# A gated mix taken in one piece, longer transfer times for a list scheduler, one weight ring for two stages, and constants set up earlier

## The chip, the cores and the metric

The kernel runs on one core of one Trainium2 chip. A core has five engines with instruction queues of their own: TensorE (PE, matmuls), VectorE (DVE), ScalarE (ACT), GpSimd (POOL) and SyncE (SP, here used only to issue transfers), and 16 DMA engines that all transfers share. The metric is the device time of one execution in microseconds (us), lower is better.

## The reference

Two branches over the same 2048 tokens of 640 values are mixed by a gate per token. Branch A is attention with a sliding window of 256 and 32 heads of 20. Branch B is a recurrence: 64 segments of 32 tokens, each with 8 memory tokens in front, 32 heads of 192, and the memory rows of one segment's output are the memory of the next.

```python
g = _sigmoid((x * gate_w).sum(-1, keepdims=True))
a = _A_ref(x, A_wqkv, A_wo)          # sliding window attention
b = _B_ref(x, B_mem0, B_Wq, B_Wk, B_Wv, B_Wo, B_seg_len)
return g * a + (1 - g) * b

# in _B_ref
for s in range(n_seg):               # 64 segments, one after the other
    h = jnp.concatenate([mem, xs], axis=1)            # 8 + 32 rows
    q = jnp.einsum('btd,dhe->bhte', h, Wq)            # k and v alike
    ...                                               # masked softmax of 40 x 40 per head
    o = jnp.einsum('bhte,hed->btd', o, Wo)
    mem = o[:, :M, :].copy()
    outs.append(o[:, M:, :])
```

## The kernel before

The program has three stages. Branch A comes first and writes its gated result `ga` to DRAM (`ga_dram`), and 1 - g (`omg`) too. The tail (`tail_projections`) then projects the last 8 tokens of all segments at once with the weights of branch B, and stores them in `xin` in DRAM. Then come 64 steps (`branch_B`), one for each segment, each of which needs the memory rows of the step before.

The four weight matrices of branch B are cut into 80 pieces of 128 x 1536 (384 KB). 58 of them stay in SBUF for good ("resident"), and 22 are read again in every step ("streamed"). `EARLY` = 33 of the resident pieces are loaded during branch A, the next 19 during the tail, and `LAST` = 6 after the tail, by ACT's queue. The streamed pieces go through a ring of `RING` = 5 buffers: SP issues a load as soon as PE has finished with the piece that held the buffer. The tail has a ring of its own (`t_ring`, 4 buffers), the steps another (`b_w`, tiles `t_w`).

The order of the steps' instructions is set by `Sched`: PE's order is written out in `STEP`, and all other operations are put in the order in which a list scheduler with durations and latencies (`LAT`, in ns) would start them. Each engine then runs its instructions in that order, and waits on semaphores for what is not ready. Transfers of the steps, except those of weights, are all issued by POOL (`hT` is a segment's input, `xqk` and `xv` are the tail's projections for it, `ga` is branch A's result).

`store(s)` is the place where the step's result is mixed. PE transposes the output of segment s (`ox`), in the middle of step s + 1; DVE mixes it with `ga` in two halves of 320 columns, and there is one buffer for `ga`:

```python
for h in range(2):
    ga, c = sc.buf("ga"), h * D // 2
    sc.op("DMA", ... dma_start(tile_of(ga)[:], ga_dram[rows, cols]), writes=[ga])   # L949
    def f_r(): nc.vector.scalar_tensor_tensor(out=ga["tile"][:], in0=ox..., in1=ga["tile"][:], ...)  # L952
    sc.op("DVE", dve(320), f_r, reads=[ox], writes=[ga])
    sc.op("DMA", ... dma_start(outf[rows, cols], ga["tile"][:]), reads=[ga])        # L955
```

So the load of one half writes the buffer that the store of the half before still reads. Other lines that the prediction speaks of: L728 projections, L873 spread of the probabilities (`PTm`, which PE's `ps_pv` at L889 needs), L917 output projection (`ps_o`), L927 the memory rows copied into the next step's input (`t_hT`, the end of one step and the start of the next), L548 and L571 matmuls of the tail, L320 and L1044 the store and the load of `omg`.

Of the kernel before, what the change touches and what calls it, by code (L numbers as in the profile page):

```python
# [8 lines left out]
FP32 = mybir.dt.float32  # L9
# [5 lines left out]
SEG = 32  # L15
# [355 lines left out]
class Sched:  # L371
# [6 lines left out]
    LAT = {"PE": 190, "DVE": 125, "ACT": 140, "POOL": 150, "DMA": 2000, "SP": 2000}  # L378
# [140 lines left out]
def tail_projections(tc, weights, xTb, xin, late):  # L519
# [6 lines left out]
    with ExitStack() as ctx:  # L526
        ring = ctx.enter_context(tc.tile_pool(name="t_ring", bufs=4))
# [5 lines left out]
        def pieces(kind, g):  # L533
            return {m: weights.get(ring, (kind, g, m)) for m in weights.order(kind, g)}
# [64 lines left out]
def branch_B(ctx, tc, xin, mem0, weights, omg_sb, ga_dram, b_dram, outf):  # L599
    nc = tc.nc  # L600
    nseg = xin.shape[0]
    scale = float(192) ** -0.5

    const = ctx.enter_context(tc.tile_pool(name="b_const", bufs=1))
    sb = {
        "w": (RING, [P, PIECE]), "tok": (3, [P, 384]), "vtok": (2, [P, 384]), "K02": (2, [P, 4, 2, L]),
        "PTm": (2, [P, 2, 4, L]), "OT": (2, [P, 3, 4, L]), "Pm": (2, [P, 4, SEG]),
        "xqk": (1, [P, 4, 2, 12, MEM]), "xv": (1, [P, 384]), "ga": (1, [SEG, D // 2]), "hT": (2, [P, KT, SEG]),
    }
    kept = {"QT": (2, [P, 12 * L + 64 - L]), "Kz": (2, [P, 4, 2, L]), "Px": (4, [P, 64]), "PTx": (4, [P, 2, 4, 2, MEM]),  # L610
            "oT": (1, [P, KT * SEG + P - SEG])}
    ps = {"mm": 3, "tr": 2, "s": 2, "o": 1}
    pools = {t: ctx.enter_context(tc.tile_pool(name=f"b_{t}", bufs=n)) for t, (n, _) in sb.items()}
    pools |= {t: ctx.enter_context(tc.tile_pool(name=f"b_ps_{t}", bufs=n, space=bass.MemoryType.PSUM)) for t, n in ps.items()}
    stats = ctx.enter_context(tc.tile_pool(name="b_stats", bufs=3))
    still = {}
    for t, (n, shape) in kept.items():
# [7 lines left out]
    mask = const.tile([P, 4, L], BF, name="bmask")  # L625
    nc.gpsimd.memset(mask[:], 0.0)
    for a in range(2):
        mk = mask[64 * a:64 * a + 64]
        nc.gpsimd.affine_select(out=mk, in_=mk, compare_op=ALU.is_ge, fill=NEG, base=0,
                                pattern=[[0, 4], [-1, L]], channel_multiplier=1)  # L630
        nc.gpsimd.memset(mask[64 * a:64 * a + MEM], 0.0)
# [7 lines left out]
    mk_h = const.tile([P, 4, 4], FP32, name="mk_h")  # L639
# [10 lines left out]
    for a in range(2):  # L650
        nc.gpsimd.memset(mk_z[64 * a:64 * a + 64, a:a + 1], 1.0)

    sc = Sched({t: n for t, (n, _) in sb.items()} | {t: n for t, (n, _) in kept.items()} | ps)

    def tile_of(b, shape=None, dtype=BF, name=None):
        t = b["tag"]
        if b["tile"] is None:
            if t in kept:
                b["tile"] = still[t][b["n"] % kept[t][0]]
            elif t in sb:  # L660
                b["tile"] = pools[t].tile(sb[t][1], BF, name=f"t_{t}", tag=t)
# [129 lines left out]
    def scores(s, g):  # L791
# [21 lines left out]
        def f1():  # L813
            x["mx"] = stats.tile([P, 4], FP32, name="sm_mx")
# [121 lines left out]
    def store(s):  # L936
# [9 lines left out]
        for h in range(2):  # L946
            ga, c = sc.buf("ga"), h * D // 2
            rows, cols = slice(s * SEG, (s + 1) * SEG), slice(c, c + D // 2)
            sc.op("DMA", 500, lambda ga=ga, rows=rows, cols=cols: nc.gpsimd.dma_start(tile_of(ga)[:], ga_dram[rows, cols]), writes=[ga])  # L949

            def f_r(ga=ga, cols=cols):
                nc.vector.scalar_tensor_tensor(out=ga["tile"][:], in0=ox["tile"][0:SEG].rearrange("p k c -> p (k c)")[:, cols],  # L952
                                               scalar=omg_sb[:, s:s + 1], in1=ga["tile"][:], op0=ALU.mult, op1=ALU.add)
            sc.op("DVE", dve(320), f_r, reads=[ox], writes=[ga])
            sc.op("DMA", 500, lambda ga=ga, rows=rows, cols=cols: nc.gpsimd.dma_start(outf[rows, cols], ga["tile"][:]), reads=[ga])  # L955
# [20 lines left out]
EARLY = 33  # L976
LAST = 6
# [4 lines left out]
def kernel(  # L982
# [40 lines left out]
    units = [lambda u=u: weights.load_resident(pre, u, nc.sync) for u in early]  # L1023
    omg_sb = fin.tile([SEG, nseg], FP32, name="omg_sb")
    with tc.tile_pool(name="b_xtail", bufs=1) as xtail:
# [17 lines left out]
        with nc.allow_non_contiguous_dma(reason="tiny omg vector"):  # L1043
            nc.sync.dma_start(omg_sb[:], omg_dram[:].rearrange("(s t) -> t s", t=SEG))  # L1044
        post = wctx.enter_context(tc.tile_pool(name="b_post", bufs=1, side="right"))
        with tc.tile_pool(name="chk", bufs=1) as chk, tc.tile_pool(name="chk_ps", bufs=1, space=bass.MemoryType.PSUM) as chk_ps:
# [51 lines left out]
```

## Time and profile before

| | us |
|---|---|
| median of 3 runs (lowest, highest) | 2730.45 (2722.23, 2738.58) |
| the profiled execution | 2727.65 |
| its span, first to last instruction | 2725.9 |
| PE busy, share of the span | 2090.3 (77%) |
| DVE busy | 1051.0 (39%) |
| ACT busy | 923.3 (34%) |
| POOL busy | 579.8 (21%) |
| DMA, mean over the span | 238 GB/s, 649.37 MB |
| chain that ended last | DMA 47%, PE 27% |

An engine's busy time is an average over three stages with different limits, so it says little about what sets the end. The chain that ended last is followed back from the last instruction, at each step to what released it; transfers make up almost half of it, those of weights and, 10% each, the load and the store of the mix. The rows below take this apart by stage.

### The profile page before, as it was taken

What the parts mean: (1) busy time and instruction counts of PE and PEld (TensorE: products, weight loads), DVE (VectorE), ACT (ScalarE), POOL (GpSimd) and SP (SyncE); (2) the same over time, 40 slices, a digit from 0 to 9 for tenths busy, and PEclk for the clock granted to TensorE, in tenths of its full rate; (3) what the DMA queues carried; (4) which work ended last, traced back from release to release, by engine and by line L of the source; (5) the groups of instructions that cost most, each with busy time, mean ns of one, the idle gap of its engine ahead of it and who ended that gap; (6) DMA issues with size and microseconds to landing.
All of it is one profiled execution on the core that took longest, in us unless ns stands there. A gap on an engine that the chain in (4) does not pass through costs nothing.

```text
span 2725.9 us, 109560 instructions
## 1 busy us (share of the span) xinstructions
PE 2090.3 (77%) x48566; PEld 1569.8 (58%) x48566; DVE 1051.0 (39%) x3330; ACT 923.3 (34%) x1957; POOL 579.8 (21%) x1752
## 2 busy tenths in 40 slices
PE   7888879977777777777777777777777777777776
PEld 6777758555555555555555555555555555555554
DVE  5666633233333333333333333333333333333333
ACT  3555522233333333333333333333333333333332
POOL 3111101231222222222222222222222222222221
PEclk8777779998898899898888888898888888888888
DMA  3211165688788777788888788888777878888876
GB/s 122 64 60 59 54 179 147 176 304 269 270 270 269 271 271 270 270 275 270 273 282 276 266 272 275 268 284 279 268 271 267 269 271 267 283 271 268 274 266 207
DMA packets 256693, 649.37 MB, mean 238 GB/s; under 512 B 38730, under 2 KB 56274, under 8 KB 256210
## 3 DMA queue, kind: packets, MB, share of 16 engines
q1 hardware_dynamic: 224754, 589.03, 63.7%
q0 software_dynamic: 25216, 47.75, 6.0%
q8 instruction: 382, 6.26, 0.9%
q10 hardware_dynamic: 6240, 5.51, 0.7%
q14 instruction: 101, 0.83, 0.1%
HBM read 612.78 MB, written 29.37 MB: 236 GB/s over the span
## 4 chain that ended last, share of the span: by engine, by line
DMA 47%; PE 27%; issue 7%; POOL 3%; DVE 2%; SPq 0%; POOLq 0%; DVEq 0%; ACT 0%; ACTq 0%
DMA t_w<-in_B_Wq_dram 13%; DMA t_ga<-ga_dram 10%; DMA out_dram<-t_ga 10%; PE ps_o L917 9%; DMA t_w<-in_B_Wv_dram 8%; DMA t_w<-in_B_Wk_dram 5%; PE ps_q L728 5%; PE t_psum L548 4%; PE ps_v L728 3%; PE ps_pv L889 2%; PE ps_k L728 1%; DVE t_PTm L873 1%; POOL b_Kz L785 1%; PE S_ps L805 1%; POOL b_QT L764 1%
## 5 line engine op out<-in xcount | busy, mean ns | idle before, releaser
L728 PEld LDWEIGHTS <-t_hT 128*32 128x32 bf16 x15360 | 384.0, 97 | 390.5 <-issue 182.9
L889 PE MATMUL ps_pv<-t_PTm,t_vtok 128*64 128x160 bf16 x1536 | 117.5, 261 | 382.9 <-DVE t_PTm L873 382.9
L917 PE MATMUL ps_o<-t_OT,w_o 128*128 128x40 bf16 x10752 | 355.0, 190 | 6.1 <-issue 5.9
L900 ACT CAST t_OT<-ps_pv 128x480 bf16<-128x480 f32 x256 | 143.8, 562 | 624.2 <-PE ps_pv L896 623.9
L917 PEld LDWEIGHTS <-w_o 128*128 128x128 bf16 x10752 | 327.3, 103 | 30.7 <-issue 23.9
L889 PEld LDWEIGHTS <-t_vtok 128*64 128x64 bf16 x1536 | 73.7, 120 | 395.8 <-issue 393.4
L952 DVE SCALAR_TENSOR_TENSOR t_ga<-ox_ps,omg_sb,t_ga 32x320 bf16<-32x320 bf16 x128 | 68.4, 534 | 517.0 <-DMA t_ga<-ga_dram 511.3
L220 ACT ACTIVATE pt<-s_ps 128x1024 bf16<-128x1024 f32 x180 | 180.7, 1023 | 126.4 <-PE s_ps L217 126.3
L764 POOL COPY b_QT<-t_xqk 128x96 bf16<-128x96 bf16 x256 | 66.8, 261 | 736.8 <-PE S_ps L805 423.4
L728 PE MATMUL ps_q<-w_q,t_hT 128*32 128x384 bf16 x3584 | 199.5, 338 | 18.8 <-DVE t_hT L927 18.4
L728 PE MATMUL ps_k<-w_k,t_hT 128*32 128x384 bf16 x4096 | 212.9, 328 | 0.0
L774 DVE COPY t_K<-tr_k 128x256 bf16<-128x256 bf16 x256 | 74.6, 292 | 335.4 <-PE tr_k L751 329.1
L728 PE MATMUL ps_v<-w_v,t_hT 128*32 128x384 bf16 x3584 | 195.5, 332 | 0.1
L738 ACT CAST t_tok<-ps_q 128x384 bf16<-128x384 f32 x256 | 122.5, 479 | 201.0 <-PE ps_q L728 195.1
L917 PE MATMUL ps_o<-t_OT,t_w 128*128 128x40 bf16 x4608 | 175.1, 189 | 9.4 <-issue 8.5
L738 ACT CAST t_vtok<-ps_v 128x384 bf16<-128x384 f32 x256 | 122.5, 478 | 172.8 <-PE ps_v L728 172.6
L738 ACT CAST t_tok<-ps_k 128x384 bf16<-128x384 f32 x256 | 122.4, 478 | 158.4 <-PE ps_k L728 156.8
L751 PEld LDWEIGHTS <-t_tok 128*64 128x64 bf16 x3072 | 103.7, 110 | 104.1 <-issue 38.9
L917 PEld LDWEIGHTS <-t_w 128*128 128x128 bf16 x4608 | 151.7, 103 | 10.8 <-issue 9.4
L873 DVE TENSOR_TENSOR t_PTm<-PT_ps,mk_m 128x320 bf16<-128x320 f32 x256 | 122.9, 480 | 80.9 <-PE PT_ps L860 77.1
L728 PE MATMUL ps_q<-t_w,t_hT 128*32 128x384 bf16 x1536 | 119.6, 330 | 43.8 <-DMA t_w<-in_B_Wq_dram 42.8
L222 DVE TENSOR_TENSOR pt<-pt,pat 128x1024 bf16<-128x1024 bf16 x180 | 124.4, 691 | 74.5 <-ACT pt L220 71.8
(133 smaller groups left out, 3697.3 us busy)
## 6 DMA issues: line engine op xcount, KB each, us to landing
t_w<-in_B_Wq_dram SPq DMA_DIRECT2D x384, 384.0 KB, 5.0
t_w<-in_B_Wv_dram SPq DMA_DIRECT2D x384, 384.0 KB, 5.2
t_w<-in_B_Wo_dram SPq DMA_DIRECT2D x384, 384.0 KB, 5.2
t_w<-in_B_Wk_dram SPq DMA_DIRECT2D x256, 384.0 KB, 4.8
xin<-t_qk POOLq DMA_DIRECT2D x8, 1536.0 KB, 9.0
t_xqk<-xin POOLq DMA_DIRECT2D x64, 192.0 KB, 5.3
w_k<-in_B_Wk_dram SPq DMA_DIRECT2D x16, 384.0 KB, 4.0
t_xv<-xin POOLq DMA_DIRECT2D x64, 96.0 KB, 2.3
```

The lines of the kernel that those rows point to most:

```text
L220: nc.scalar.activation(out=pt, in_=sp[:], func=ACT.Exp, scale=scale)
L222: nc.vector.tensor_tensor(out=pt, in0=pt, in1=pat.unsqueeze(1).to_broadcast([P, 2, 512]), op=ALU.min)
L548: nc.tensor.matmul(pt[:, bb, :], lhsT=w[kt][:, c:c + P], rhs=xTb[:, kt, t0:t0 + HS * MEM], start=(x == 0), stop=(x == KT - 1))
L728: nc.tensor.matmul(t[32 * j:32 * j + 32, 0:384], lhsT=tile_of(hT)[:, kt, :], rhs=w[:, j * 384:(j + 1) * 384], start=(x == 0), stop=(x == K ...
L738: nc.scalar.copy(dst, src)
L751: nc.tensor.transpose(t[64 * a:64 * a + 64, k, :], tok["tile"][:, c:c + 64], ident[:], tile_position=(0, 64 * a))
L764: nc.gpsimd.tensor_copy(dst, tile_of(xqk)[:, g, 0, :, :])
L774: nc.vector.tensor_copy(tile_of(K02)[:, :, :, 0:SEG], src)
L873: nc.vector.tensor_tensor(out=tile_of(PTm)[:], in0=src.to_broadcast([P, 2, 4, L]), in1=mk_m[:].unsqueeze(1).unsqueeze(3).to_broadcast([P, ...
L889: nc.tensor.matmul(t[64 * a:64 * a + 64, 160 * b:160 * b + 160], lhsT=V["tile"][:, c:c + 64], rhs=PTm["tile"][:, a, :, :].rearrange("p j l ...
L900: sc.op("ACT", act(480), lambda: nc.scalar.copy(tile_of(OT)[:].rearrange("p b j l -> p (b j l)"), o["tile"][:, 0:480]), reads=[o], writes= ...
L917: nc.tensor.matmul(t[:, dt * L:(dt + 1) * L], lhsT=w_of("o", g, m, wb)[:, c:c + P], rhs=OT["tile"][:, b, i, :], start=(g == 0 and n == 0), ...
```

## The change

In a step, the mix is one operation over 640 columns in one buffer of that width, with one load and one store. `LAT` gives a transfer 5000 instead of 2000, and SP's weight loads 2500 instead of 2000. The tail and the steps share one ring of five buffers, created before branch A, and the streamed pieces of the first head group are loaded into it at the end of branch A (`first`). To make room, `EARLY` goes from 33 to 28 and `LAST` from 6 to 8, so that 22 resident pieces are loaded in the tail. The constants of the steps (zeroed buffers, identity, masks) are set up before the tail, not after it. The load of `omg` and the store of the range flag go from SP's queue to POOL's. The score mask is kept once and broadcast to the four heads, and three small softmax tiles become one with two buffers instead of three.

```diff
-    LAT = {"PE": 190, "DVE": 125, "ACT": 140, "POOL": 150, "DMA": 2000, "SP": 2000}
+    LAT = {"PE": 190, "DVE": 125, "ACT": 140, "POOL": 150, "DMA": 5000, "SP": 2500}
...
-def tail_projections(tc, weights, xTb, xin, late):
+def tail_projections(tc, weights, ring, first, xTb, xin, late):
...
-        ring = ctx.enter_context(tc.tile_pool(name="t_ring", bufs=4))
...
-            return {m: weights.get(ring, (kind, g, m)) for m in weights.order(kind, g)}
+            return {m: first.pop((kind, g, m), None) or weights.get(ring, (kind, g, m)) for m in weights.order(kind, g)}
...
+def step_constants(tc, const, tmp):
...
-    mask = const.tile([P, 4, L], BF, name="bmask")
+    mask = const.tile([P, 1, L], BF, name="bmask")
...
-        "xqk": (1, [P, 4, 2, 12, MEM]), "xv": (1, [P, 384]), "ga": (1, [SEG, D // 2]), "hT": (2, [P, KT, SEG]),
+        "xqk": (1, [P, 4, 2, 12, MEM]), "xv": (1, [P, 384]), "ga": (1, [SEG, D]), "hT": (2, [P, KT, SEG]),
...
+    pools["w"] = ring
...
-                nc.tensor.matmul(t[64 * a:64 * a + 64, 0:4 * L], lhsT=ident[:, 64 * a:64 * a + 64],
-                                 rhs=mask[:].rearrange("p j l -> p (j l)"), start=True, stop=False,
+                nc.tensor.matmul(t[64 * a:64 * a + 64, 0:4 * L].rearrange("p (j l) -> p j l", j=4), lhsT=ident[:, 64 * a:64 * a + 64],
+                                 rhs=mask[:].to_broadcast([P, 4, L]), start=True, stop=False,
...
-        for h in range(2):
-            ga, c = sc.buf("ga"), h * D // 2
-            rows, cols = slice(s * SEG, (s + 1) * SEG), slice(c, c + D // 2)
-            sc.op("DMA", 500, lambda ga=ga, rows=rows, cols=cols: nc.gpsimd.dma_start(tile_of(ga)[:], ga_dram[rows, cols]), writes=[ga])
...
-            sc.op("DVE", dve(320), f_r, reads=[ox], writes=[ga])
-            sc.op("DMA", 500, lambda ga=ga, rows=rows, cols=cols: nc.gpsimd.dma_start(outf[rows, cols], ga["tile"][:]), reads=[ga])
+        ga, rows = sc.buf("ga"), slice(s * SEG, (s + 1) * SEG)
+        sc.op("DMA", 500, lambda: nc.gpsimd.dma_start(tile_of(ga)[:], ga_dram[rows, :]), writes=[ga])
...
+        sc.op("DVE", dve(640), f_r, reads=[ox], writes=[ga])
+        sc.op("DMA", 500, lambda: nc.gpsimd.dma_start(outf[rows, :], ga["tile"][:]), reads=[ga])
...
-EARLY = 33
-LAST = 6
+EARLY = 28
+LAST = 8
...
+    ring = wctx.enter_context(tc.tile_pool(name="b_w", bufs=RING))
+    first = {}
+    ahead = [("q", 0, m) for m in range(5)] + [("k", 0, m) for m in range(5)]
+    ahead = [u for u in ahead if u in weights.streamed]
+
+    def load_first(u):
+        first[u] = weights.get(ring, u)
+    units += [lambda u=u: load_first(u) for u in ahead]
...
-            nc.sync.dma_start(omg_sb[:], omg_dram[:].rearrange("(s t) -> t s", t=SEG))
+            nc.gpsimd.dma_start(omg_sb[:], omg_dram[:].rearrange("(s t) -> t s", t=SEG))
...
+            step_c = step_constants(tc, bconst, chk)
...
-            nc.sync.dma_start(flag_dram[:], flag[:])
+            nc.gpsimd.dma_start(flag_dram[:], flag[:])
```

POOL's queue in the second half of a step, before, where all transfers around the mix are issued (`out_dram` is the store of a mixed piece, `t_ga` the load of the next):

```order
L955 DMA out_dram<-t_ga 32x320
L676 DMA t_hT<-xin 128x160
L949 DMA t_ga<-ga_dram 32x320
L955 DMA out_dram<-t_ga 32x320
L686 DMA t_xv<-xin 128x384
L949 DMA t_ga<-ga_dram 32x320
L945 DMA b_dram<-b_oT_8458 128x160
```

The same place of a step in the changed kernel (in every other step the load of `b_hT` stands ahead of the store):

```order
L966 DMA out_dram<-b_ga 32x640
L690 DMA b_hT<-xin 128x160
L700 DMA b_xv<-xin 128x384
L960 DMA b_ga<-ga_dram 32x640
L958 DMA b_dram<-b_oT_6452 128x160
```

One store and one load are left of two each, and the load is that of the next step's mix: it stands behind the store of this step's.

DVE's queue around the mix, before (the rows are those of one step; `t_PTm` is what PE's next matmuls with the values need):

```order
L952 SCALAR_TENSOR_TENSOR t_ga<-ox_ps,omg_sb,t_ga 32x320
L873 TENSOR_TENSOR t_PTm<-PT_ps,mk_m 128x320
L825 TENSOR_REDUCE sm_sum<-S_ps 128x4
L868 TENSOR_TENSOR b_PTx_8452<-PT_ps,mk_x 64x128
L829 RECIPROCAL sm_rs<-sm_sum 128x4
L836 TENSOR_TENSOR t_Pm<-S_ps,sm_rs 128x128
L840 TENSOR_TENSOR b_Px_8445<-S_ps,sm_rs 128x32
L952 SCALAR_TENSOR_TENSOR t_ga<-ox_ps,omg_sb,t_ga 32x320
L873 TENSOR_TENSOR t_PTm<-PT_ps,mk_m 128x320
```

and in the changed kernel:

```order
L963 SCALAR_TENSOR_TENSOR b_ga<-ox_ps,omg_sb,b_ga 32x640
L839 TENSOR_REDUCE sm<-S_ps 128x4
L886 TENSOR_TENSOR b_PTm<-PT_ps,mk_m 128x320
L842 RECIPROCAL sm<-sm 128x4
L881 TENSOR_TENSOR b_PTx_6446<-PT_ps,mk_x 64x128
L849 TENSOR_TENSOR b_Pm<-S_ps,sm 128x128
L853 TENSOR_TENSOR b_Px_6439<-S_ps,sm 128x32
L886 TENSOR_TENSOR b_PTm<-PT_ps,mk_m 128x320
```

The second mix, which stood ahead of the step's last `PTm`, is gone; the one mix stands where the first half's did. Apart from the mixes and their transfers, the steps' rows of ACT and SP stand in the same order in both kernels, and those of DVE and POOL too but for a few neighbours that change places.

SP's queue where branch A ends and the tail begins, before (`w_ring` are streamed pieces, `w_v` and the like resident ones):

```order
L193 DMA ga_dram<-ga 128x640 x3
L320 DMA omg_dram<-omg_all 128x16x1
L1049 DMA flag_dram<-flag 1x1
L493 DMA w_v_6538<-in_B_Wv_dram 128x1536
L1044 DMA omg_sb<-omg_dram 32x64x1
L493 DMA w_ring<-in_B_Wq_dram 128x1536 x2
L493 DMA w_ring<-in_B_Wk_dram 128x1536
```

and in the changed kernel:

```order
L493 DMA w_ring<-in_B_Wq_dram 128x1536
L193 DMA ga_dram<-ga 128x640
L493 DMA w_ring<-in_B_Wq_dram 128x1536
L493 DMA w_ring<-in_B_Wk_dram 128x1536
L493 DMA w_ring<-in_B_Wq_dram 128x1536 x2
L193 DMA ga_dram<-ga 128x640 x3
L320 DMA omg_dram<-omg_all 128x16x1
L493 DMA w_k_6586<-in_B_Wk_dram 128x1536
```

The first five streamed pieces now stand ahead of the store of `omg`, and the load of `omg` no longer stands on this queue.

## Rows read from the trace of the kernel before

**Rows 1.** The page's first line.

```profile
span 2725.9 us, 109560 instructions
```

**Rows 2.** Instructions of line L927, the copy that ends a step.

```profile
L927 DVE CAST t_hT<-ps_o x63: 198/199/200, 581.7 to 2681.7; 128x40 bf16<-128x40 f32 x63
```

**Rows 3.** PE's waits, 582 to 2682 us: waiter, releaser, total us, times, longest.

```profile
PE ps_pv L889 <- DVE t_PTm L873: 379.1, 62, 8.4
PE ps_q L728 <- DMA t_w<-in_B_Wq_dram: 41.8, 69, 3.2
PE ps_k L728 <- DMA t_w<-in_B_Wk_dram: 34.4, 58, 2.0
PE ps_v L728 <- DMA t_w<-in_B_Wv_dram: 31.6, 50, 2.1
```

**Rows 4.** DVE's timeline of one step: start, duration, [idle before, releaser].

```profile
1546.88 0.53 DVE L952 SCALAR_TENSOR_TENSOR t_ga<-ox_ps,omg_sb,t_ga 32x320 bf16<-32x320 bf16 x1
...
1557.66 0.54 DVE L952 SCALAR_TENSOR_TENSOR t_ga<-ox_ps,omg_sb,t_ga 32x320 bf16<-32x320 bf16 x1 [8.66 <-DMA t_ga<-ga_dram]
```

**Rows 5.** POOL's timeline of the same step.

```profile
1547.70 0.51 POOL L955 DMA_DIRECT2D out_dram<-t_ga  x1 [0.24 <-DVE t_ga L952]
...
1553.15 0.51 POOL L949 DMA_DIRECT2D t_ga<-ga_dram  x1 [4.38 <-DMA out_dram<-t_ga]
1558.49 0.50 POOL L955 DMA_DIRECT2D out_dram<-t_ga  x1 [4.83 <-DVE t_ga L952]
```

**Rows 6.** Stretches: engines' busy us, then granted clock, DMA share, GB/s.

```profile
554.00:582.00 28.00, 25.43 (x667) 17.61 (x668) 11.43 (x43) 10.53 (x25) 10.04 (x43) 0.91 1.00 357
566.00:602.00 36.00, 32.06 (x867) 22.40 (x856) 18.21 (x68) 15.59 (x38) 8.42 (x33) 1.00 0.96 336
640.00:2680.00 2040.00, 1525.53 (x39989) 1120.27 (x39989) 723.20 (x2583) 640.78 (x1501) 454.39 (x1442) 0.88 0.80 271
1552.00:1558.60 6.60, 0.09 (x4) 0.11 (x1) 0.94 (x2) 0.00 (x0) 0.62 (x2) 0.77 0.58 203
1558.60:1563.50 4.90, 4.61 (x132) 4.44 (x131) 0.49 (x2) 0.56 (x1) 1.10 (x3) 0.62 0.36 87
380.00:390.00 10.00, 10.00 (x72) 8.01 (x71) 3.78 (x10) 2.62 (x9) 0.00 (x0) 0.76 1.02 385
```

**Rows 7.** Transfers between 566 and 592 us.

```profile
DMA packets 3250, 8.86 MB, mean 341 GB/s; under 512 B 403, under 2 KB 419, under 8 KB 3243
```

**Rows 8.** Pieces of the chain that ended last: start, duration, what.

```profile
554.49 1.79 PE ps_q L728 x20
...
574.38 1.60 PE ps_o L917 x60
...
1526.07 3.66 PE ps_o L917 x120
...
1530.00 1.03 PE ps_q L728 x20
```

**Rows 9.** The same chain, end of branch A.

```profile
361.77 12.06 DMA omg_dram<-omg_all
```

**Rows 10.** PE's timeline, start of the tail and of step 0.

```profile
378.72 1.55 PE L548 MATMUL t_psum<-xTb,w_ring 128*128 128x256 bf16 x6 [14.25 <-DMA w_ring<-in_B_Wq_dram]
...
544.96 0.49 PE L571 MATMUL t_psv<-w_ring,xTb 128*128 128x384 bf16 x2
553.79 0.27 PE L711 MATMUL tp<-ident,t_w 8*128 8x8 bf16 x5 [8.35 <-POOL ident masks.py:199]
```

**Rows 11.** SP's timeline ahead of step 0: the step's first streamed pieces.

```profile
495.92 0.81 SPq L493 DMA_DIRECT2D t_w<-in_B_Wq_dram  x2
...
504.32 0.43 SPq L493 DMA_DIRECT2D t_w<-in_B_Wk_dram  x1
```

**Rows 12.** Timeline of the end of the span.

```profile
2712.95 0.54 DVE L952 SCALAR_TENSOR_TENSOR t_ga<-ox_ps,omg_sb,t_ga 32x320 bf16<-32x320 bf16 x1 [5.60 <-PE ox_ps L943]
...
2720.64 0.50 POOL L955 DMA_DIRECT2D out_dram<-t_ga  x1 [3.29 <-DVE t_ga L952]
```

More of the change, by code (lines that the diff above doesn't have):

```diff
@@ L596 @@
 STEP = "q0 k1 tq0 q1 k0 tq1 tk1 k2 tk0 q3 s0 s1 v0 q2 tk2 v1 tq2 p0 k3 p1 s2 tq3 pv0 tk3 v2 pv1 s3 x p2 v3 o0 p3 pv2 o1 pv3 o2 o3"
-def branch_B(ctx, tc, xin, mem0, weights, omg_sb, ga_dram, b_dram, outf):
-    nc = tc.nc
[L601 to L607, printed above, removed]
-        "xqk": (1, [P, 4, 2, 12, MEM]), "xv": (1, [P, 384]), "ga": (1, [SEG, D // 2]), "hT": (2, [P, KT, SEG]),
[L609 to L615, printed above, removed]
+KEPT = {"QT": (2, [P, 12 * L + 64 - L]), "Kz": (2, [P, 4, 2, L]), "Px": (4, [P, 64]), "PTx": (4, [P, 2, 4, 2, MEM]),
+        "oT": (1, [P, KT * SEG + P - SEG])}
+class Constants:
+    pass
+def step_constants(tc, const, tmp):
+    nc = tc.nc
     still = {}
-    for t, (n, shape) in kept.items():
+    for t, (n, shape) in KEPT.items():
         still[t] = [const.tile(shape, BF, name=f"b_{t}{i}") for i in range(n)]
@@ L638, in branch_B @@
                             pattern=[[SEG, 4]], channel_multiplier=-1)
-    mk_h = const.tile([P, 4, 4], FP32, name="mk_h")
+    mk_h = tmp.tile([P, 4, 4], FP32, name="mk_h")
     nc.gpsimd.memset(mk_h[:], 1.0)
@@ L651, in branch_B @@
         nc.gpsimd.memset(mk_z[64 * a:64 * a + 64, a:a + 1], 1.0)
+    c = Constants()
+    c.still, c.ident, c.mask, c.mk_m, c.mk_x, c.mk_z = still, ident, mask, mk_m, mk_x, mk_z
+    return c
+def branch_B(ctx, tc, xin, mem0, weights, ring, c, omg_sb, ga_dram, b_dram, outf):
+    nc = tc.nc
+    nseg = xin.shape[0]
+    scale = float(192) ** -0.5
+    still, ident, mask, mk_m, mk_x, mk_z = c.still, c.ident, c.mask, c.mk_m, c.mk_x, c.mk_z
+    kept = KEPT
+    sb = {
+        "w": (RING, [P, PIECE]), "tok": (3, [P, 384]), "vtok": (2, [P, 384]), "K02": (2, [P, 4, 2, L]),
+        "PTm": (2, [P, 2, 4, L]), "OT": (2, [P, 3, 4, L]), "Pm": (2, [P, 4, SEG]),
+        "xqk": (1, [P, 4, 2, 12, MEM]), "xv": (1, [P, 384]), "ga": (1, [SEG, D]), "hT": (2, [P, KT, SEG]),
+    }
+    ps = {"mm": 3, "tr": 2, "s": 2, "o": 1}
+    pools = {t: ctx.enter_context(tc.tile_pool(name=f"b_{t}", bufs=n)) for t, (n, _) in sb.items() if t != "w"}
+    pools["w"] = ring
+    pools |= {t: ctx.enter_context(tc.tile_pool(name=f"b_ps_{t}", bufs=n, space=bass.MemoryType.PSUM)) for t, n in ps.items()}
+    stats = ctx.enter_context(tc.tile_pool(name="b_stats", bufs=2))
     sc = Sched({t: n for t, (n, _) in sb.items()} | {t: n for t, (n, _) in kept.items()} | ps)
@@ L660, in tile_of @@
             elif t in sb:
-                b["tile"] = pools[t].tile(sb[t][1], BF, name=f"t_{t}", tag=t)
+                b["tile"] = pools[t].tile(sb[t][1], BF, name=f"b_{t}", tag=t)
             else:
@@ L813, in f1 @@
         def f1():
[L814 removed]
+            sm = stats.tile([P, 4, 4], FP32, name="sm")
+            x["mx"], x["sum"], x["rs"] = sm[:, 0], sm[:, 1], sm[:, 2]
             nc.vector.tensor_reduce(out=x["mx"][:], in_=view(), axis=AX.X, op=ALU.max)
@@ L1055 @@
             weights.load_resident(rest, u, nc.scalar)
-        branch_B(bctx, tc, xin, mem0, weights, omg_sb, ga_dram, b_dram, outf)
+        branch_B(bctx, tc, xin, mem0, weights, ring, step_c, omg_sb, ga_dram, b_dram, outf)
     wctx.close()
```

15 lines of the change are left out of this document (7 added, 8 removed).

## The prediction

> **What bounds the kernel now.** I read the span first and cut it by stage. The copy of the memory rows ends each step; it starts 63 times, first at 581.7 and last at 2681.7 us [rows 2]. That makes 62 periods of 33.87 us, 2100 of the span's 2725.9 us [rows 1, 2]. What is left is 581.7 us ahead and 44.2 us behind. So one microsecond in a step is worth 62, and one elsewhere is worth one.
>
> Next I read PE's waits over these periods, because PE's order is fixed and every step ends with it. PE waited 379.1 us for `PTm` on DVE, once a step and 6.1 us each, and 107.8 us (41.8 + 34.4 + 31.6) for weight pieces, 1.7 us a step [rows 3]. `PTm` itself is short. DVE's timeline shows what held it: the second half of the mix stands ahead of it and sat 8.66 us waiting for the load of `ga` [rows 4]. POOL's timeline shows why the load was late: the first half's store was issued at 1547.70, the next load wants the same buffer, so POOL waited for the store to land and issued the load at 1553.15 [rows 5]. A store and a load, one after the other, stand on PE's path in each step.
>
> Last I asked what is next in line when this wait is gone. The steps move 271 GB/s on the mean [rows 6], which is 271 x 33.87 us = 9.18 MB a step. While PE stands still (1552 to 1558.6) the five ring buffers fill, and then the queue has nothing to do: DMA share 0.58 there and 0.36 in the 4.9 us after it, so some 6 us of a step's transfer time go unused [rows 6]. The first two steps show the kernel without this wait, since step 0 has no mix and the first half of the mix in step 1 had its load long done: from 566 to 602 us the DMA share is 0.96 and the rate 336 GB/s [rows 6], 341 in its first 26 us [rows 7]. There the transfers set the pace.
>
> **The whole mix and its times.** The change removes 64 DVE operations, 64 loads and 64 stores. POOL no longer issues two of them per step at 0.51 us [rows 5]; POOL waits more than it works, so I count nothing. The mix itself doubles in columns: 0.53 us for one half [rows 4], so between 0.53 and 1.07 us for the whole. I take 1.07; it adds up to 0.5 us ahead of a `PTm` that PE wants only after a projection and the first output projection (1.60 us for 60 matmuls [rows 8]), so nothing on the path. The load that mattered now stands behind the store of the step before, and its mix comes half a step or more later: a store and a load took 5.45 us (1547.70 to 1553.15) and 4.51 us (to the mix at 1557.66) [rows 4, 5], about 10 together, against some 20 us from the store to the next mix even if a step shrinks. Hence no wait. POOL's wait for the store is covered too, because the load of `xv` that stands between needs the step's last matmuls with the values. The larger latency numbers do nothing but put the rows in this order.
>
> What is late next is a weight piece. A step's 9.18 MB at 336 GB/s takes 27.3 us. PE alone needs less: 33.87 - 6.1 - 1.7, and 0.8 for the clock, is 25.3 us. The last term comes from the half clock after the idle stretch (granted 0.77 and 0.62 of 2.4 GHz [rows 6]): 120 output matmuls took 3.66 us there and 2 x 1.60 otherwise, and I round up for the matmuls ahead of them [rows 8]. So the period goes from 33.87 to 27.3 us, and 62 x 6.57 = 407 us are saved.
>
> By the Trainium skill's "DMA: Bandwidth & Descriptors", section Specifications, HBM gives a core about 358 GB/s, and its section Bandwidth has 425 for large transfers of a core alone. With the first a step's bytes would take 25.6 us, with the second 21.6, less than PE needs. This trace shows 385 GB/s over 10 us of weight loads [rows 6], above the first figure; the steps, with their small transfers in between, showed 336 when nothing else held them.
>
> **The ring, the preloads and the queue.** At the end of branch A SP waited for the store of `omg` (12.06 us [rows 9]) before it could load the tail's first streamed pieces, and PE waited 14.25 us for them [rows 10]. Now five pieces are loaded ahead and the load of `omg` waits on POOL, where the next thing that matters is a store of the tail some 20 us of PE work later. That is worth 14.3 us, with 10 as a floor if something else holds the tail's start.
>
> At the other end of the tail PE idled 8.35 us until POOL had set up the identity [rows 10]. With the constants there, up to 8.35 us could go. But the first steps are paced by transfers (share 1.00 from 554 to 582 [rows 6]), and these get more: the old kernel had four of step 0's pieces loaded ahead of time (first at 495.92, last at 504.32 [rows 11]), and the shared ring has room for two of them while the tail's last pieces are in use; and eight resident pieces instead of six come after the tail. Four pieces of 0.393 MB at 341 GB/s are 4.6 us. Of the difference of 3.8 I count 2. The bounds for the whole start are a gain of 8 and of 22 us; I take 16.
>
> **The end.** From the last copy of L927 to the mix behind it the old kernel took 31.25 us [rows 2, 12], of which I put 1.2 down to the copy and transposes in between; a last step of 27.3 us saves 2.7. Behind it, the old kernel goes from the first half's mix at 2712.95 through store, load and second mix to the last store at 2720.64 [rows 12]; the new one issues its only store some 1.4 us after the mix's start (1.07 for the mix and 0.29 from a mix's end to its store [rows 4, 5]), so 6.3 us less. Together 9.
>
> **Small edits.** The broadcast mask feeds eight score matmuls a step with the same columns, and the merged softmax tile is written and read by DVE alone, in order. I count nothing. If the broadcast read at half speed, PE would lose less than 1 us a step, since a whole projection of 20 wider matmuls takes 1.03 [rows 8], and the transfers cover that up to 27.3.
>
> **Sum.** 2725.9 - 407 - 16 - 9 = 2293.9 us of span; the profiled execution's time is 1.75 us above its span, so about 2295 us, and this execution (2727.65) lies 0.1% below the median of the runs.
>
> **Rivals.**
> *PE sets the pace.* If the loads run at the 357 GB/s of step 0 [rows 6], a step's bytes take 25.7 us, and PE's 25.3 is the bound. 62 x 8.57 = 531 us saved gives 2171. For it: nothing in 566 to 602 is free of the start's extra loads. Against: the 336 there. 0.13. By the figure of 425 GB/s of the page named above it would come out this way.
> *Both bounds add.* With 25.3 and 27.3 so close, PE's pauses leave the ring full at times and PE waits for pieces at others. If the present 1.7 us of weight waits come on top, a step takes 29 us and the time is 2400; up to 31 us, 2525. For it: PE waited for weights in nearly every step even with a ring that had just been filled. Against: 0.96 of DMA share between 566 and 602 with such pauses in it. 0.22.
> *The change doesn't do what it says.* Another late transfer takes the place of `ga` in each step, for instance `xqk`, and a step stays over 31 us: 2525 to 2720. Against: no order but the mix's changes, and PE shows no other wait of a transfer. 0.05, a third of it within half a per cent.
> *Slower: half clock in every step.* PE would pause for pieces in 22 places of a step instead of once. If the granted clock then stayed at its lower level, a projection takes 1.79 instead of 1.03 us [rows 8]; with projections near 10 us of a step this and the rest at half speed make PE's 25.3 about 39, and the time 2295 + 62 x 11.7 = 3020. It turns slower from the point where some six tenths of a step run at half clock. Against: the granted clock was 1.00 from 566 to 602, with such pauses; it fell in the one long pause [rows 6]. By the Trainium skill's "TensorE: Matmul & The Clock Gate", section on HAM oscillation, waits for transfers between bursts of matmuls are what drops this clock; the trace agrees for the long pause alone. 0.03.
>
> **How the numbers follow.** My forecast, transfers setting the pace at 26.2 to 28.4 us (2227 to 2363), gets 0.57. The range reaches half into the faster case (25.6 us) and over half into the one above (29.5 us): 2190 to 2430 us, which leaves out about 0.2. The three runs lie within 0.3% of their median, so half a per cent is about what a measurement can tell from no change. Faster 0.95, same 0.02, slower 0.03.
>
> **What would show it.** PE's waits for `PTm` should be gone and those for weight pieces grow to 2 us a step or more. The copies of L927 (now L940) should stand about 27.3 us apart, DMA share in the steps near 0.96, granted clock near 1.00. DVE should show no wait for `ga`, and PE's 14.25 us ahead of the tail should be gone. I am wrong if DVE or POOL shows a new wait once a step, or if the rate in the steps settles away from 336 GB/s with the share still near 1.

## The result and the profile after

The change makes the kernel faster: a median of 2388.09 us over 4 runs (2374.79 to 2395.13) against 2734.51 us for the kernel before on the same chip (4 runs), a ratio of 0.872 (95% interval 0.866 to 0.879). The direction was forecast and the range holds the time, but it lies 93 us above the forecast of 2295. The profiled execution took 2395.13 us, the longest of the four.

The first lines of the page of the changed kernel (to set beside [rows 1]), with the slices of TensorE's clock and of the DMA engines:

```profile
span 2393.4 us, 109199 instructions
...
PE 2065.2 (86%) x48566; PEld 1518.5 (63%) x48566; DVE 1041.4 (44%) x3266; ACT 923.5 (39%) x1957; POOL 513.7 (21%) x1626
...
PEclk8777768998999999999999999999999999999999
DMA  3122117559999999999999999999999999999998
```

The copy that ends a step, now L940, in the same kernel (beside [rows 2]):

```profile
L940 DVE CAST b_hT<-ps_o x63: 198/199/200, 582.2 to 2359.4; 128x40 bf16<-128x40 f32 x63
```

The period is (2359.4 - 582.2) / 62 = 28.66 us; 27.3 was forecast and 33.87 measured before. With it the span falls apart into the same three parts as before. The steps gave back 62 x 5.21 = 323 us of the forecast 407. Ahead of the first copy nothing was gained (582.2 after 581.7) where 16 us were forecast. Behind the last copy 34.0 us are left of 44.2, a gain of 10.2 where 9 was forecast. The misfits of +85 (1.365 us times 62), +16.5 and -1.2 us make up the difference between 2393.4 and the 2293.9 of the sum to within a microsecond.

PE's waits in the changed kernel between 582 and 2360 us (beside [rows 3]): waiter, releaser, total us, times, longest.

```profile
PE ps_o L930 <- issue: 68.3, 67, 2.5
PE ps_k L742 <- DMA b_w<-in_B_Wk_dram: 46.2, 63, 2.6
PE ps_v L742 <- DMA b_w<-in_B_Wv_dram: 35.5, 51, 1.9
PE ps_q L742 <- DMA b_w<-in_B_Wq_dram: 32.9, 58, 2.0
...
PE ps_o L930 <- DMA b_w<-in_B_Wo_dram: 8.8, 19, 0.7
```

The wait for `PTm` is gone, and DVE has no wait for `ga` any more. The waits for weights grew little, from 107.8 to 114.6 us for the three projections, 1.85 us a step where 2 or more were forecast. The longest row is new in kind: before the output projection PE stood still for 68.3 us in 67 places with nothing in the profile that released it ("issue"). The kernel before had 10.5 us of these in its steps between 700 and 1980 us.

Stretches of the changed kernel (beside [rows 6]): the steps, the 7.3 us ahead of step 0, and step 0.

```profile
640.00:2340.00 1700.00, 1475.31 (x39415) 1050.52 (x39408) 703.06 (x2486) 633.79 (x1484) 384.30 (x1303) 0.97 0.94 321
538.60:545.90 7.30, 0.30 (x9) 0.24 (x13) 1.85 (x4) 1.75 (x4) 2.02 (x4) 0.66 0.63 201
545.90:582.40 36.50, 28.09 (x660) 18.46 (x660) 11.17 (x41) 10.44 (x24) 8.81 (x32) 0.83 0.97 349
```

The reader should hold on to 0.94 of DMA share at 321 GB/s in the steps. It looks as if transfers set the pace, as forecast, only more slowly than 336 GB/s. A rate that settles away from 336 with the share still near 1 was one of the prediction's own signs of being wrong, and the experiments show that this reading is wrong.

### The profile page after: what moved, and what is told of

Read it like the earlier page. It is cut to its first block, busy times and chain, and to the rows that moved or that the text cites. A ratio compares the mean times of both kernels' runs of the same rounds, so it can differ in the third digit from the quotient of the medians.

```text
span 2393.4 us, 109199 instructions
## 1 busy us (share of the span) xinstructions
PE 2065.2 (86%) x48566; PEld 1518.5 (63%) x48566; DVE 1041.4 (44%) x3266; ACT 923.5 (39%) x1957; POOL 513.7 (21%) x1626
## 4 chain that ended last, share of the span: by engine, by line
PE 49%; DMA 38%; issue 6%; ACT 3%; DVE 3%; POOL 0%; SPq 0%; ACTq 0%; DVEq 0%; POOLq 0%
PE ps_o L930 13%; DMA b_w<-in_B_Wq_dram 13%; DMA b_w<-in_B_Wv_dram 10%; DMA b_w<-in_B_Wk_dram 8%; PE ps_q L742 6%; DMA b_w<-in_B_Wo_dram 5%; PE qk_ps L132 5%; PE ps_v L742 5%; PE ps_k L742 4%; PE t_psum L547 4%; ACT pt L220 2%; PE ps_pv L902 2%; PE s_ps L217 2%; PE S_ps L819 1%; DMA xin<-t_vt 1%
## 5 line engine op out<-in xcount | busy, mean ns | idle before, releaser
L742 PEld LDWEIGHTS <-b_hT 128*32 128x32 bf16 x15360 | 388.0, 98 | 415.9 <-issue 214.2
L930 PE MATMUL ps_o<-b_OT,w_o 128*128 128x40 bf16 x10752 | 327.3, 181 | 49.5 <-issue 49.0
L913 ACT CAST b_OT<-ps_pv 128x480 bf16<-128x480 f32 x256 | 143.8, 562 | 233.1 <-PE ps_pv L909 232.9
L742 PE MATMUL ps_k<-w_k,b_hT 128*32 128x384 bf16 x4096 | 225.3, 339 | 4.3 <-issue 4.3
L742 PE MATMUL ps_q<-w_q,b_hT 128*32 128x384 bf16 x3584 | 203.8, 343 | 20.9 <-DVE b_hT L940 18.4
L742 PE MATMUL ps_v<-w_v,b_hT 128*32 128x384 bf16 x3584 | 195.5, 332 | 0.3 <-ACT b_tok L752 0.3
L930 PE MATMUL ps_o<-b_OT,b_w 128*128 128x40 bf16 x4608 | 167.2, 181 | 32.1 <-issue 22.3
L940 DVE CAST b_hT<-ps_o 128x40 bf16<-128x40 f32 x63 | 12.5, 199 | 403.7 <-PE ps_o L930 403.7
L886 DVE TENSOR_TENSOR b_PTm<-PT_ps,mk_m 128x320 bf16<-128x320 f32 x256 | 124.7, 487 | 133.8 <-PE PT_ps L873 129.9
L930 PEld LDWEIGHTS <-b_w 128*128 128x128 bf16 x4608 | 140.8, 97 | 38.8 <-issue 26.1
L742 PE MATMUL ps_q<-b_w,b_hT 128*32 128x384 bf16 x1536 | 125.9, 346 | 35.0 <-DMA b_w<-in_B_Wq_dram 33.3
```

What stands on the lines that cost most here:

```text
L742: nc.tensor.matmul(t[32 * j:32 * j + 32, 0:384], lhsT=tile_of(hT)[:, kt, :], rhs=w[:, j * 384:(j + 1) * 384], start=(x == 0), stop=(x == K ...
L886: nc.vector.tensor_tensor(out=tile_of(PTm)[:], in0=src.to_broadcast([P, 2, 4, L]), in1=mk_m[:].unsqueeze(1).unsqueeze(3).to_broadcast([P, ...
L913: sc.op("ACT", act(480), lambda: nc.scalar.copy(tile_of(OT)[:].rearrange("p b j l -> p (b j l)"), o["tile"][:, 0:480]), reads=[o], writes= ...
L930: nc.tensor.matmul(t[:, dt * L:(dt + 1) * L], lhsT=w_of("o", g, m, wb)[:, c:c + P], rhs=OT["tile"][:, b, i, :], start=(g == 0 and n == 0), ...
```

## The experiments

Between 700 and 1980 us every kernel below is in its steps; stretches named without a window are this one. Periods are worked out as above, from the first and last of the 63 copies. The share of the DMA engines adds up the times of packets and can pass 1. This stretch of the kernel before and of the changed kernel (us, then busy us and count of PE, PEld (TensorE's weight loads), DVE, ACT and POOL, granted clock, DMA share, GB/s):

```profile
700.00:1980.00 1280.00, 960.25 (x25270) 705.80 (x25270) 456.91 (x1633) 405.25 (x950) 287.16 (x912) 0.89 0.81 273
700.00:1980.00 1280.00, 1112.39 (x29729) 791.91 (x29718) 534.37 (x1889) 477.82 (x1119) 291.51 (x989) 0.97 0.94 322
```

### The other edits without the whole mix

The changed kernel with the two half buffers, their loads and stores, and the old latency numbers.

```diff
-    LAT = {... "DMA": 5000, "SP": 2500}
+    LAT = {... "DMA": 2000, "SP": 2000}
-        ga, rows = sc.buf("ga") ...          # one buffer of 640 columns
+        for h in range(2): ga, c = sc.buf("ga"), h * D // 2 ...
```

> The changed kernel with the mix in two halves and the scheduler's old times again; ring, preloads, constants, mask and softmax tile stay changed. If the mix alone made the steps shorter, DVE's wait for ga (about 8 us a step) is back, the copies that end a step stand 33.6 to 34.1 us apart and the time is 2710 to 2740 us. If the one ring or the preloads had a part in it, the period is under 33 us and the time under 2680.

Measured: 2723.08 us over 10 runs, ratio 0.9975 (0.9942 to 1.0008). The copies stand 33.76 us apart (576.7 to 2669.7) against 33.87, with DVE's wait for `ga` in place, as its waits between 582 and 2300 us show:

```profile
DVE b_ga L965 <- DMA b_ga<-ga_dram: 408.0, 51, 9.6
```

So the shared ring, the preloads, the constants, the mask and the merged softmax tile are worth nothing in a step as long as the mix stands there in halves. The first copy comes 5 us earlier in the profiled execution, a size that the whole time can't tell from nothing. The whole mix without these other edits was not run.

### The whole mix with the old times

```diff
-    LAT = {... "DMA": 5000, "SP": 2500}
+    LAT = {... "DMA": 2000, "SP": 2000}
```

> The changed kernel with the scheduler's old transfer times (2000, 2000) alone put back; the load of ga then stands right behind the store, ahead of the load of xv. If the whole buffer is what counts, DVE does not wait for ga here either, POOL waits some 4 us a step for the store with nothing urgent behind it, the period stays at 28.4 to 29.0 us and the time at 2370 to 2405. If the longer times are needed, POOL's wait holds the loads behind it, a wait of 1 us or more a step shows on PE, and the time is 2450 or more.

Measured: 2376.52 us, ratio 0.872 (0.866 to 0.878), the same as the whole change; the copies stand 28.43 us apart (577.6 to 2340.5). The longer times given to the scheduler are not needed: POOL waits 4.6 us a step for the store (279.6 us in 61 places between 582 and 2340 us), and no wait on PE follows from it. This run and the one before differ in the mix alone, so the whole buffer makes the gain.

### The flag in a place of its own

In the changed kernel the tail's first casts wait for a tiny store. PE's timeline there (beside [rows 10]), with the idle time ahead in brackets:

```profile
376.84 0.27 PE L547 MATMUL t_psum<-xTb,w_ring 128*128 128x256 bf16 x1
382.97 1.01 PE L547 MATMUL t_psum<-xTb,w_k 128*128 128x256 bf16 x4 [5.86 <-ACT t_qk L552]
```

and DVE's:

```profile
382.16 2.74 DVE L554 CAST t_qk<-t_psum 128x256 bf16<-128x256 f32 x8 [15.91 <-DMA flag_dram<-flag]
```

PE's 14.25 us for weights are gone, as forecast, but PE fills the PSUM banks and stops after all. The buffers that the casts write (`t_stage`) take the place in SBUF of the pool that holds `flag`, and its store, issued at 368.59, 2.1 us after the store of `omg`, took 13.4 us to land. In this run the tile was moved:

```diff
-        flag = chk.tile([1, 1], mybir.dt.int32, name="flag")
+        flag = fin.tile([1, 1], mybir.dt.int32, name="flag")
```

> The changed kernel with the range flag's tile kept for good, so that no later tile takes its place while its store is under way. If the store of the flag on POOL's queue (13.4 us to landing) is what holds the first casts of the tail, DVE's wait of 15.9 us and PE's of 5.9 us there are gone, and the time falls by 5 to 7 us, 0.2 to 0.3%. If the casts wait for something else that ends as late, for instance the load of omg on the same queue, the waits stay and the time with them.

Measured: 2389.22 us, ratio 0.873 (0.868 to 0.879). PE's wait shrank only from 5.86 to 4.09 us, because DVE's found the next store, in its timeline:

```profile
375.52 2.74 DVE L554 CAST t_qk<-t_psum 128x256 bf16<-128x256 f32 x8 [12.29 <-DMA omg_dram<-omg_all]
```

A wait of this size can't be told in the whole time, and PE's wait itself was 7.4 us in the runs with the old times and with eight ring buffers, which leave the flag where it was. What the trace tells is that the store of `omg`, for which SP waited before and POOL's load waits now, still holds the tail through a third engine, DVE. The casts don't use `omg`; that they want the place of its tile, as with the flag, is read from this wait.

### Eight ring buffers

Three resident pieces are not loaded, and other pieces are read in their place; their room goes to the ring. Bytes and matmuls of a step stay the same.

```diff
-RING = 5
+RING = 8
+    gone, early = early[-3:], early[:-3]     # get() hands out another piece for these
...
```

> The changed kernel with eight ring buffers instead of five; to make room, three resident pieces are not loaded and others are used in their place, so every matmul and every streamed load is as it was but three preloads. Theory one, the transfers set the pace: the queue already moves what it can, the period stays within 0.3 us of 28.7 and the time at 2370 to 2400. Rival, the ring is too short: PE and the queue wait for each other in turns, with eight buffers the share of DMA goes from 0.94 to 0.97 or more, the period falls to 27.3 us or less and the time to 2305 or less.

Measured: 2328.83 us, ratio 0.853 (0.849 to 0.857), between the two expectations. The stretch:

```profile
700.00:1980.00 1280.00, 1123.24 (x30600) 805.73 (x30601) 540.74 (x1933) 491.49 (x1152) 298.86 (x1012) 0.96 0.95 331
```

and PE's longest waits in it:

```profile
PE ps_o L932 <- issue: 84.6, 72, 3.1
PE ps_q L744 <- DVE b_hT L942: 13.4, 46, 0.3
PE S_ps L821 <- issue: 9.3, 14, 1.2
```

The period is 27.75 us (577.0 to 2297.6). PE waits for no weight piece any more, so it is not the landing of pieces that holds it, and still a step takes 4.3 us more than PE needs alone (23.46 us, measured next). Waits without a releaser take the place of those for weights.

### Each bound alone

First PE without streamed loads: every streamed piece is replaced by a resident one, with the same matmuls. Then the loads with less PE work: of each projection only the matmuls that read streamed pieces are run, with five buffers and with eight.

```diff
 # PE alone
-            if u in weights.streamed:
+            if False:
...
 # loads with less PE work
+            ks = [kt for kt in ks if kt in wb] or ks[-1:]
...
```

> The changed kernel without the streamed weight loads in the steps; a resident piece stands in for each, so PE's work and order are unchanged and the other transfers stay. It measures what PE and its chain need by themselves: 25.3 us a step was the estimate, which gives a time near 2180 us. If PE's chain alone takes 27 us or more, the transfers are not what the period of 28.7 us consists of.

> The changed kernel with every streamed load, but without the matmuls on resident pieces where a chunk has a streamed one, so PE has roughly half its work. Five ring buffers. Theory one, the transfers can do no more than about 321 GB/s with this mix: the period stays at 28 us or more. Rival, PE and the queue wait for each other: with PE early at every piece a buffer is free again at once, the period falls to 27 us or less, which at 9.2 MB a step is 340 GB/s or more.

> As the run before, with eight ring buffers: the most that the transfers of a step can do when neither PE nor a buffer holds them. With eight buffers and full PE work the period was 27.75 us at 332 GB/s. If that was the transfers' own limit, it stays at 27.2 to 27.9 us here; if PE's pauses still cost something there, it falls to 26.5 us or less.

Measured: 2058.35, 2277.78 and 2036.11 us, one run each. The stretch of PE alone:

```profile
700.00:1980.00 1280.00, 1260.70 (x36324) 923.08 (x36320) 638.92 (x2292) 580.51 (x1363) 354.48 (x1200) 1.00 0.09 24
```

of less PE work with five buffers:

```profile
700.00:1980.00 1280.00, 950.72 (x15490) 585.02 (x15489) 560.70 (x2002) 513.76 (x1188) 309.85 (x1048) 0.56 0.96 341
```

and with eight:

```profile
700.00:1980.00 1280.00, 1020.88 (x18028) 643.46 (x18024) 644.17 (x2330) 593.89 (x1384) 359.68 (x1221) 0.65 1.03 396
```

PE alone needs 23.46 us a step (copies from 571.9 to 2026.6), not 25.3. With less PE work a step takes 26.82 us with five buffers (580.3 to 2243.3) and 23.11 with eight (572.1 to 2004.7). In both the second of the two expectations holds. So 336 to 341 GB/s, at a share of 0.96, was the rate of a ring of five that PE reads and no limit of the transfers: with eight the same loads moved 396 GB/s. PE was no quick reader in these two runs: its granted clock was 0.56 and 0.65, mostly the lower of its two levels (1.2 and 2.4 GHz), and it was busy for 74% and 80% of the stretch. What the loads do with no reader at all is measured below.

### Smaller pieces

The same bytes in halves of 192 KB through ten half buffers (and the flag as above).

```diff
-        "w": (RING, [P, PIECE])               # 5 x 1536 columns
+        "w": (RING, [P, HALF])                # 10 x 768 columns
...
```

> The changed kernel, complete, with the streamed pieces loaded in halves of 128 x 768 (192 KB) into ten buffers of half the size, and the flag's tile kept as in the run for it. The ring takes the same room, but half a piece is free again as soon as its matmuls are done. If waiting for whole buffers is part of what a step costs, the period falls by 0.3 to 0.9 us, to 27.8 to 28.4 us, and the time to 2325 to 2370. If the smaller loads cost more per byte, or SP's 44 issues a step get in the way, the period rises above 28.7 and the time above 2390.

Measured: 2432.37 us, ratio 0.891 (0.886 to 0.896): slower than the change. The copies stand 29.38 us apart (573.0 to 2394.5), at 313 GB/s and a share of 0.95. A half took 4.4 to 4.7 us to land where a whole piece took 5.1 to 5.3. The second expectation holds; whether the smaller loads or SP's 44 issues a step cost the time is not shown.

### Loads that nobody reads

All streamed pieces are loaded, but PE reads resident pieces as in the run of PE alone. PE then waits for no load, and no load for PE. Five buffers, then eight (three pieces not loaded).

```diff
-        return out
+        return {}
...
```

> Part left out: the matmuls read resident pieces wherever a streamed one stands in the changed kernel, as in the run without loads, but the streamed pieces are all loaded, into five ring buffers that nobody reads. So PE never waits for a piece, and the loads never wait for PE. Theory A (the loads slow PE's own stream while they run, which shows as idle time that the profile puts down to no releaser): the period rises from 23.46 us to 25.5 to 27 us, with 2 us a step or more of such idle time, most of it ahead of the output projection. Theory B (PE loses time only by its waits for pieces and for a ring that fills and empties in turn): the period stays within 23.4 to 24 us and such idle time stays near nothing.

> Part left out: as in the run before, with eight ring buffers (three resident pieces not loaded, others in their place). The loads then run nearer to 396 GB/s than to 341. Theory A: the idle time that no releaser explains grows with the rate, and the period lies above that of the run with five buffers, 26 to 28 us. Theory B: 23.4 to 24 us, as with five.

Measured: 2363.28 and 2464.41 us, one run each. The stretch with five buffers, and PE's longest wait in it, which again has no releaser:

```profile
700.00:1980.00 1280.00, 1106.46 (x29663) 787.57 (x29659) 520.55 (x1865) 476.44 (x1114) 289.90 (x980) 0.94 1.00 366
PE ps_o L930 <- issue: 106.2, 73, 2.9
```

and with eight:

```profile
700.00:1980.00 1280.00, 1039.09 (x26760) 735.66 (x26755) 471.77 (x1682) 429.42 (x1002) 260.82 (x882) 0.91 1.03 394
PE ps_o L932 <- issue: 130.6, 75, 2.9
```

The copies of the run with eight, between 700 and 1980 us and, in the second row, after the loads had ended:

```profile
L942 DVE CAST b_hT<-ps_o x40: 198/199/200, 711.1 to 1950.5; 128x40 bf16<-128x40 f32 x40
L942 DVE CAST b_hT<-ps_o x13: 198/199/200, 2151.3 to 2432.8; 128x40 bf16<-128x40 f32 x13
```

While the loads run, a step takes 28.67 us at 366 GB/s (five buffers, 44 periods from 706.7 to 1968.2) and 31.78 us at 394 (39 periods). In the same run with eight buffers it takes 23.46 us again once they have ended (12 periods). Theory A holds, and more strongly than I had written: loads that PE doesn't touch cost it 5.2 to 8.3 us a step. And five buffers that nobody reads move 366 GB/s, not 341: the 341 was the pace of ring and reader together.

Where PE stands still tells why. The stretches below, of the run with eight buffers, each reach from the end of one such wait to the end of the next:

```profile
953.20:959.50 6.30, 4.67 (x127) 3.39 (x128) 4.24 (x15) 1.71 (x4) 2.69 (x10) 0.99 1.02 390
959.50:965.70 6.20, 4.72 (x128) 4.44 (x128) 0.79 (x2) 1.12 (x2) 1.07 (x2) 0.73 1.02 390
965.70:971.95 6.25, 4.97 (x128) 3.85 (x127) 0.20 (x1) 0.77 (x2) 0.57 (x1) 0.73 1.02 387
...
990.35:996.55 6.20, 3.81 (x128) 3.55 (x128) 0.79 (x2) 1.12 (x2) 1.07 (x2) 1.00 1.04 400
```

Between two waits lie 128 matmuls and 128 weight loads, whatever they compute (a record is missing here and there), and 6.2 us (the median of 139 such stretches between 700 and 1980 us; the least is 4.8 and the most 6.6). Where waits stand farther apart, it is by two, three or four times that number. The DMA queue q8, named "instruction", moves packets of just that size. Its row in the changed kernel, packets, MB and share:

```profile
q8 instruction: 233, 3.82, 1.1%
```

3.82 MB over the 29729 matmuls and 29718 weight loads of that stretch are 64 bytes for each, and a packet of 16.4 KB holds 256. So PE's own instructions come through the same 16 DMA engines, a packet for each 128 matmuls, 5.2 packets a step. At 4.5 us of PE work to a packet (23.46 / 5.2) DMA engines with little else to move, 24 GB/s, deliver them in time; at 394 GB/s they come 6.2 us apart, and 5.2 x 6.2 = 32 us is about the measured step.

That the waits are for these packets shows in the traces' records of the packets themselves: each of the 66 waits without a releaser that PE has in the changed kernel in this stretch ends 1.1 to 1.6 us after the end of a packet of q8, and so does each of the 169 of the run with eight buffers (1.2 to 1.6 us). And the runs with less PE work changed the number of instructions. The row of q8 in the one with eight buffers:

```profile
q8 instruction: 141, 2.31, 0.7%
```

There PE took 9.1 us to a packet (1280 / 141), and at 396 GB/s not one of its waits is without a releaser. With the same rate of transfers and a packet wanted every 4.5 us, the run with eight unread buffers has 169.

### One buffer more or less, for one piece

Complete kernels that trade a ring buffer against a resident piece.

```diff
-RING = 5
-EARLY = 28
+RING = 4                                       # or 6
+EARLY = 29                                     # or 27
-STREAMED = {... "o": (1, 2, 2, 1)}
+STREAMED = {... "o": (1, 1, 2, 1)}             # or (2, 2, 2, 1)
```

> The whole computation. One ring buffer less, and in its room one more piece kept resident (an output piece of group 2): 21 pieces loaded per step instead of 22, 8.79 MB instead of 9.18. Theory A (the bytes moved in a step count, by their own time and by the pace that they leave to PE's instruction stream): the period falls by about 4%, from 28.7 to 27.5 us, and the time to 2310 to 2350 us. Theory B (the ring's round trip counts: four buffers on their way move less per microsecond than five, as five moved less than eight): the rate in the steps falls from 322 to about 300 GB/s, the period rises to 29 us or more, and the time to 2390 to 2450 us.

> The whole computation. The same trade the other way: six ring buffers, one resident piece fewer (an output piece of group 0), 23 pieces and 9.57 MB per step. Theory A: the period rises by about 4%, to 29.8 us, and the time to 2440 to 2470 us. Theory B: the rate rises to about 345 GB/s or more, the period falls to 28.3 us or less, and the time to 2330 to 2370 us.

Measured: 2552.89 us with four (ratio 0.935, 0.932 to 0.939) and 2385.02 with six (0.873, 0.869 to 0.876). The stretch with four buffers:

```profile
700.00:1980.00 1280.00, 1059.29 (x27478) 743.40 (x27478) 490.08 (x1725) 440.37 (x1028) 268.44 (x905) 0.95 0.87 284
```

and with six:

```profile
700.00:1980.00 1280.00, 1124.64 (x29840) 800.62 (x29837) 530.07 (x1889) 477.94 (x1120) 293.50 (x990) 0.95 0.96 336
```

With four, theory B holds and was too mild: 31.11 us a step (578.3 to 2506.9) at 284 GB/s, though fewer bytes are moved. With six the step takes 28.55 us (579.3 to 2349.3): the rate rises, the waits for weights fall to 30.5 us in the stretch, and the waits without a releaser before the output projection grow from 47.9 to 84.3. Both theories missed there, since the gain of the one is given back to the other. No complete kernel that I ran is shown to beat the changed one.

## Why the prediction was right, and where it failed

The direction and most of the gain came by the mechanism that was forecast. That the range holds the time owes something to luck: the forecast's own case, transfers setting the pace, ended at 28.4 us a step and 2363 us, and the measured 28.66 us and 2388 us lie above it, in the part of the range that was kept for a rival.

**The mix: right.** The store and the load were PE's wait of each step; with them out of the way both DVE's and PE's wait are gone, and the rest of the change alone is worth nothing in a step. On POOL no new wait holds PE: its wait ahead of the load of `xv` grew from 44.4 to 209.2 us over the steps, but it is one for PE's own matmuls, as forecast. The latency numbers did nothing, as forecast. The load of `ga` lands with no wait on DVE.

**"There the transfers set the pace": the step that failed.** The forecast took 336 GB/s at a share of 0.96 [rows 6] for the limit of the transfers, and so 27.3 us for the period. It was what five buffers move with PE as their reader; five that nobody reads moved 366, and the same loads reached 396 with eight. And it took the larger of two bounds, 27.3 and 25.3, as if each left the other alone. Measured apart they are 25.1 us (a step's 9.18 MB at 366 GB/s) and 23.5, and together 28.66. The rival "both bounds add", with 29 us and 2400, came closer. Between 700 and 1980 us the changed kernel's step splits as follows, with 44.7 steps in the stretch: PE busy 24.9 us (1112.4 / 44.7) against 23.1 in the run of PE alone, waits for weights 1.9, waits without a releaser 1.4, and 0.3 for the copy of the memory rows, 28.5 together. The rival's own term, 1.7 us of weight waits on top, is met by the 1.9, but the 27.3 that it adds them to is no part of the step. What neither had is the instruction stream. It accounts for the 1.4 us directly, and for part of the 1.8 us of longer busy time if the clock dropped behind its pauses: windows that begin at such a wait have granted clocks of 0.73 as well as 1.00 above. By an estimate from the granted clock of 0.97, which takes all of the missing clock as lost by a busy PE, that part is at most 0.03 x 28.66 = 0.9 us. In the run with five unread buffers the same estimate gives 0.06 x 28.67 = 1.7 us, all of the 1.7 us by which PE is busy longer there. The other 0.9 us may come with the waits for pieces, which that run doesn't have; no run shows it, and this stays open.

**PE's own need: mis-sized.** 25.3 us was read from the steps before by taking known waits away; 23.46 was measured. The term that was too small is the clock's: 0.8 us were taken off for it, from two groups of matmuls, but PE was busy 25.4 us a step in the kernel before (960.25 us in 37.8 steps) and 23.1 in the run of PE alone, 2.3 us less. The granted clock was 0.88 over those steps [rows 6] and 1.00 in PE alone.

**The start: mis-sized.** Of 16 us nothing came in the profiled execution, and 4 to 6 in the first four runs above, whose start is the same or nearly so (first copies at 576.1 to 577.6). The wait for the tail's weights went, but the floor named for it, 10 us if something else holds the start, was too high: 5.86 us of PE's wait stayed, behind the stores of branch A. Branch A itself ended 4.7 us later in that execution (the store of `omg` was issued at 366.51 in place of 361.77). At the other end PE's 8.35 us became 6.69 us for ACT's last casts of the tail:

```profile
545.28 0.27 PE L725 MATMUL tp<-ident,b_w 8*128 8x8 bf16 x5 [6.69 <-ACT t_vt L575]
```

And step 0, which begins at 545.87 in place of 554.49, takes 36.3 us and gives these 8.6 us back. That is the four extra pieces of the forecast and more: the eight resident pieces on ACT's queue took 8.1 us each to land, and ACT's first cast of the step stood behind them, from ACT's timeline:

```profile
552.08 0.48 ACT L752 CAST b_tok<-ps_q 128x384 bf16<-128x384 f32 x1 [6.90 <-DMA w_o<-in_B_Wo_dram]
```

PE waited 3.3 us for this cast and 2.5 us without a releaser in step 0, and its granted clock was 0.83 there, against 0.91 before [rows 6]. The forecast counted these loads by their bytes alone, not by what is queued behind their issue.

**The end: right.** One mix and one store are left, 10.2 us less where 9 was forecast (beside [rows 12]). DVE's timeline has the mix:

```profile
2387.61 0.87 DVE L963 SCALAR_TENSOR_TENSOR b_ga<-ox_ps,omg_sb,b_ga 32x640 bf16<-32x640 bf16 x1 [6.22 <-PE ox_ps L956]
```

and POOL's the store:

```profile
2388.78 0.51 POOL L966 DMA_DIRECT2D out_dram<-b_ga  x1 [0.85 <-DVE b_ga L963]
```

The mix of 640 columns takes 0.87 us, between the bounds of 0.53 and 1.07.

**The slower rival: not seen as a state of the whole step.** The granted clock over the steps rose to 0.97. A clock that stays low does occur in this case: with about half of PE's matmuls in a step and five buffers it was 0.56. The rival's 39 us don't follow from its own words: 10 us of projections times 1.79 / 1.03, and twice the other 15.3, make 48.

## What to carry to other kernels

A DMA share near 1 doesn't say that transfers are the limit: eight buffers instead of five raised the rate from 341 to 396 GB/s while the share went from 0.96 to 1.03, so vary the number of buffers on their way before taking a rate for a bound. Two bounds that lie close together don't make a time that is the larger of the two; measure each alone, then both at once with the coupling taken out, as with loads that nobody reads. And when an engine stands still with no releaser, count its instructions between two such waits, and look for a transfer that ends just before each.

## What the hardware showed that was not expected

PE's instructions arrive in packets of 256 (16.4 KB, a matmul and its weight load for two of them), through the DMA engines that carry the data. Waiting for them cost nothing at 24 GB/s of other traffic, 0.3 us a step at 273 GB/s (10.5 us of waits in 37.8 steps before the output projection), and 31.78 - 23.46 = 8.3 us a step at 394 GB/s, the slower clock behind the pauses included. With a packet wanted only every 9.1 us they cost nothing even at 396 GB/s. Most of these waits stand before the short 128 x 40 matmuls of the output projection: 47.9 of 62.8 us in the changed kernel.

One piece of 384 KB took 5.1 us to land with five buffers and 7.3 to 7.5 us with eight, while the rate rose from 341 to 396 GB/s (the runs with less PE work).
